# Seven products in place of eight for two token blocks of a second expert mixture

## The chip, the cores and the metric

One core of one Trainium2 chip runs the whole kernel in one launch. The metric is the device time in microseconds of a run; the kernel before has a median of 664.22 us over three runs (663.23 to 666.79).

## The reference

Three stages follow one another, in fp32. An attention with two kinds of masks (half of the heads local, half strided) gives 1152 tokens of 512 values. Then come two feed-forward mixtures:

```
h = np.maximum(x @ w_in, 0.0);  x = h * h @ w_out          # 512 -> 2048 -> 512, w_in and w_out given as float64
p = domain_probs / (domain_probs.sum(-1, keepdims=True) + 1e-09)
for e in range(4):                                        # 512 -> 1024 -> 512 for each expert
    h = np.maximum(x @ w1[e], 0.0)
    out += p[:, e:e + 1] * (h @ w2[e])
```

The second mixture runs all four experts on all tokens, so it is four dense feed-forward layers. Its first products, `x @ w1[e]`, are what the change works on.

## The kernel before

**Tiling.** The 1152 tokens are three blocks of `TB` = 384. Features are taken 128 at a time ("feature tile"); the 512 model values are `KD` = 4 contraction tiles of 128. A weight "unit" holds two feature tiles: for `w1` 512 x 256 values, for `w2` 256 x 512. An expert has four units of each.

**Precision.** Every operand is kept as a high and a low half (`fp32r` tiles of shape [128, 2, ...]); each product is three matmuls, high x high, high x low and low x high (`mm3`, lines 587 to 590). ScalarE makes the high half with a copy, VectorE the low half as value minus high half. For weights this is `hi` (L565) and `lo` (L569, on POOL for the first mixture and on VectorE for the second), for hidden tiles `hi` (L638) and `lo` (L641), which both read the accumulator tile of the first product and apply the ReLU.

**Order of the second mixture.** `steps` (line 258) lists expert, block and feature tile, with blocks in the order 2, 1, 0. One step is a first product, 4 contraction tiles x 3 matmuls of 384 columns into a tile `bh` of a ring of two (lines 606 to 618), then high and low half of the hidden tile. Two steps later (`LAG` = 2) comes its second product: for each of three groups of 128 tokens, three matmuls of 512 columns into accumulators `by`/`ba` that run over all eight feature tiles (lines 694 to 714, L710 to L712). Then VectorE adds the accumulator, times the expert's probability, into `acc` (`gather`, L723 and L725), and after the last expert the rows are stored. `RUN` = 2: two first products, then two second products, in turn.

```
steps += [(2, e, b, i) for e in range(E) for b in (2, 1, 0) for i in range(n2)]
r = (n - moe1) % RUN
return due(n - r) + 10 * r
```

**The end of the first mixture.** Its phases are `(block, half of the features)`; the last two are block 1 and block 0, second half. Their result is the sum of the accumulator and a `spill` tile of the first half (`both`, L679, written in place), and then `x` gets a high half (L684) and a low half (L687).

**What sets the order.** The class `Plan` takes every piece of work as a task with an engine, an estimated duration (`mm_r`, `act`, `dve`, `pool`, `dma`, lines 231 to 250), a rank, the tasks it comes after and the buffers that it takes from or gives back to rings. `run` (line 70) simulates the engines: whenever one is idle it starts the ready task of lowest rank whose buffers are free. The instructions are emitted in that order, each engine works its own list in that order, and the real waits are semaphores. All loads are issued from SP's queue. The weight ring `w` has 10 tiles and 3 more (`W_LATE`) when attention's memory is given up in `open_late` (line 504); the ring `raw` for loaded weights has 3.

Of the kernel before, what the change touches and what calls it, by code (L numbers as in the profile page):

```python
# [7 lines left out]
F32 = mybir.dt.float32  # L8
# [4 lines left out]
ALU = mybir.AluOpType  # L13
# [26 lines left out]
class Plan:  # L40
# [6 lines left out]

    SAME, CROSS, DMA = 100, 200, 2200
# [5 lines left out]
    def __init__(self):  # L54
        self.tasks, self.rings = [], {}
        self.filler = None

# [3 lines left out]
    def add(self, engines, emit, after=(), rank=0, take=(), free=(), adds=(), behind=None):  # L61
# [4 lines left out]
        t.number, t.begin, t.end, t.behind = len(self.tasks), None, None, behind  # L66
        self.tasks.append(t)
        return t

    def run(self):  # L70
# [21 lines left out]
        while done < len(self.tasks):  # L92
# [25 lines left out]
            for e in ready:  # L118
                while idle[e] and ready[e]:
                    held, got = [], None  # L120
                    while ready[e]:
                        item = heapq.heappop(ready[e])
                        t = item[2]
                        if t.begin is not None:
                            continue
                        if all(any(self.rings[r] for r in rings) for _, _, rings in t.take):
                            got = t
                            break
                        held.append(item)
# [27 lines left out]
def tile_attention_mlp_experts(ctx: ExitStack, tc: tile.TileContext, a, out):  # L157
# [7 lines left out]
    banks = ctx.enter_context(tc.tile_pool(name="banks", bufs=1, space=PSUM))  # L165
    attn = ExitStack()
# [3 lines left out]
    def f32(x):  # L170
        return x.bitcast(F32)

# [23 lines left out]
    RUN = 2  # L196
# [7 lines left out]
    W_EARLY, W_LATE = 10, 3  # L204
# [7 lines left out]
    spill = many(main, "y", NB - 1, [P, KD, TB])  # L212
    plan.ring("w", many(main, "w", W_EARLY, [P, 2, 4 * CH], F32R))
    plan.ring("raw", many(main, "raw", NRAW, [P, 4 * CH], U32))
    plan.ring("mid", many(main, "mid", NMID, [P, 2 * CH]))
    plan.ring("val", many(main, "val", NMID, [P, 2 * CH]))
    plan.ring("hid", many(main, "h", NHID, [P, 2, TB], F32R))
    plan.ring("r", many(main, "r", 2, [P, TB]))
# [20 lines left out]

    def act(n):  # L240
        return n + 40
# [16 lines left out]
    steps += [(2, e, b, i) for e in range(E) for b in (2, 1, 0) for i in range(n2)]  # L258
    n_steps = len(steps)
# [5 lines left out]
    grouped = moe1 + RUN  # L265

    def turn(n):

        r = (n - moe1) % RUN
        return due(n - r) + 10 * r  # L270

    def in_unit(st, e, i):
        return ("wi" if st == 1 else "w1", e, i * P // CH)

    def out_unit(st, e, i):
        return ("wo" if st == 1 else "w2", e, i * P // CH)
# [227 lines left out]
    def open_late(e):  # L504
# [3 lines left out]
        for s in range(W_LATE):  # L508
            late["w", s] = lp.tile([P, 2, 4 * CH], F32R, name=f"wl{s}")

    t_late = plan.add({"none": 1}, open_late, after=attention_done, rank=0, adds=[("w", [("w", s) for s in range(W_LATE)])])


    first, last_use = {}, {}
    for n, (st, e, b, i) in enumerate(steps):
        for u, k in ((in_unit(st, e, i), n), (out_unit(st, e, i), n + LAG)):
            first.setdefault(u, k)
            last_use[u] = n
    w_env, w_ready = {}, {}

    def weights(u):
        env = w_env[u]
        w = env["w"]
        return late[w] if isinstance(w, tuple) else w

    chain = {"dma": None, "w": None}
    for u in sorted(first, key=lambda x: first[x]):
# [3 lines left out]
        rank = due(first[u]) - (CONV0 if first[u] <= LAG else CONV)  # L531
        for j in range(2):
# [39 lines left out]
            if first[u] > LAG or wide_:  # L572
                chain["dma"] = t
# [6 lines left out]
            t = plan.add({"act": act(n)}, hi, after=[t, chain["w"]], rank=rank + 2000, take=[(w_env[u], "w", ["w"])] if j == 0 else [])  # L580
            chain["w"] = t
            lo_engines = {"pool": pool(n)} if wide_ else {"dve": dve(n)}
            t = plan.add(lo_engines, lo, after=[t], rank=rank + R_LO, free=[(env, "val") if wide_ else (env, "raw")])
# [7 lines left out]

    spare = plan.rings["bank_y"].pop()
    phase_of = {p: k for k, p in enumerate(phases)}
    whole = {b: phase_of[b, 1] == phase_of[b, 0] + 1 for b in range(NB)}
    x2_ready = {}
    spilled = {}
    y_env = {}
    use = {}
    previous = previous_y = None
    for n in range(n_steps + LAG):  # L600
        if n < n_steps:
            st, e_, b, i = steps[n]
            env = use[n] = {}
            u = in_unit(st, e_, i)
            order = (2, 3, 0, 1)
            for pos, kk in enumerate(order):
                def product(e, env=env, u=u, b=b, i=i, kk=kk, pos=pos):
                    w = weights(u).rearrange("p s (k f) -> p s k f", k=KD)
# [3 lines left out]
                if st == 1:  # L612
                    x_in = x_ready[b, (0, 1) if kk < 2 else (2, 3)]
                else:
                    x_in = [x2_ready[b, kk]]
                freed = [(w_env[u], "w")] if pos == 3 and last_use[u] == n else []
                previous = plan.add({"pe": 3 * mm_r(TB)}, product, after=[previous if pos else None, *x_in, *w_ready[u]], rank=due(n) + pos * PE_SLICE if n < grouped else turn(n) + pos, behind=previous if n >= grouped else None, take=[(env, "H", ["bank_h"])] if pos == 0 else [], free=freed, adds=[("bank_y", [spare])] if n == 0 and pos == 0 else ())
            t = previous
            rank = due(n) - URGENT
            if st == 1:  # L620
                def relu(e, env=env):
                    nc.scalar.activation(out=env["r"], in_=env["H"][:, :TB], func=AF.Relu, scale=1.0 / WSCALE)  # L622

                def square(e, env=env):
                    h = env["H"][:, :TB]
                    nc.vector.scalar_tensor_tensor(out=h, in0=h, scalar=0.0, in1=env["r"], op0=ALU.max, op1=ALU.mult)  # L626

                def hi(e, env=env):
                    nc.scalar.activation(out=env["hid"][:, 0], in_=env["H"][:, :TB], func=AF.Copy)  # L629

                def lo(e, env=env):
                    nc.vector.tensor_tensor(out=env["hid"][:, 1], in0=env["H"][:, :TB], in1=f32(env["hid"][:, 0]), op=ALU.subtract)  # L632

                t = plan.add({"act": act(TB)}, relu, after=[t], rank=rank, take=[(env, "r", ["r"])])
                t = plan.add({"dve": dve(TB)}, square, after=[t], rank=rank, free=[(env, "r")])
            else:
                def hi(e, env=env):
                    nc.scalar.activation(out=env["hid"][:, 0], in_=env["H"][:, :TB], func=AF.Relu)  # L638

                def lo(e, env=env):  # L640
                    nc.vector.scalar_tensor_tensor(out=env["hid"][:, 1], in0=env["H"][:, :TB], scalar=0.0, in1=f32(env["hid"][:, 0]), op0=ALU.max, op1=ALU.subtract)  # L641

# [5 lines left out]
        st, e_, b, i = steps[n]  # L648
        env = use[n]
        u = out_unit(st, e_, i)  # L650
        rank = due(n + LAG) + R_OUT
        freed_w = [(w_env[u], "w")] if last_use[u] == n else []
        if st == 1:
            hh = i // half
            start = i == (0 if whole[b] else hh * half)
            stop = i == n1 - 1 or (not whole[b] and i == half - 1)
            for d in range(KD):
                if start:
                    y_env[d] = {}

                def product(e, env=env, u=u, i=i, d=d, y=y_env[d], start=start, stop=stop):
                    w = weights(u).rearrange("p s (k f) -> p s k f", k=2)
                    cs = slice(d * P, (d + 1) * P)
                    mm3(y["y"][:, :TB], w[:, 0, i % 2, cs], w[:, 1, i % 2, cs], env["hid"][:, 0], env["hid"][:, 1], start, stop)

                freed = [(env, "hid"), *freed_w] if d == KD - 1 else []
                t = previous_y = plan.add({"pe": 3 * mm_r(TB)}, product, after=[env["ready"], previous_y, *w_ready[u]], rank=rank + d * PE_SLICE, take=[(y_env[d], "y", ["bank_y"])] if start else [], free=freed)
                if not stop:
                    continue
                y = y_env[d]  # L670
                if hh == 0:
                    def keep(e, b=b, d=d, y=y):
                        nc.scalar.activation(out=spill[b][:, d], in_=y["y"][:, :TB], func=AF.Copy)

                    spilled[b, d] = plan.add({"act": act(TB)}, keep, after=[t], rank=rank, free=[(y, "y")])
                    continue
                if not whole[b]:
                    def both(e, b=b, d=d, y=y):
                        nc.vector.tensor_tensor(out=y["y"][:, :TB], in0=y["y"][:, :TB], in1=spill[b][:, d], op=ALU.add)  # L679

                    t = plan.add({"dve": dve(TB)}, both, after=[t, spilled[b, d]], rank=rank)

                def hi(e, b=b, d=d, y=y):
                    nc.scalar.activation(out=xt[b][:, 0, d], in_=y["y"][:, :TB], func=AF.Copy, scale=1.0 / WSCALE**2)  # L684

# [139 lines left out]
```

## Time and profile before

| | |
|---|---|
| median of three runs | 664.22 us (663.23 to 666.79) |
| the profiled execution | 663.53 us |
| its span, first to last instruction | 661.8 us |
| TensorE busy | 648.0 us, 98% of the span, 3964 matmuls |
| VectorE, ScalarE, POOL busy | 278.7, 201.1, 57.7 us |
| granted TensorE clock, mean | 0.997 |
| moved over HBM | 42.13 MB read, 2.36 MB written |

How to read it: "busy" is the union of an engine's instructions in time. Matmuls overlap in the records (one of 384 columns has a duration of about 0.33 us and the next starts 0.17 us later), so the spacing of starts, not the duration, is what a matmul costs in a full stream. PEld is TensorE's loading of the stationary operand, which goes on beside it. A number behind an arrow names what ended an engine's idle time. Granted clock 1.00 is 2.4 GHz, the upper of TensorE's two levels; the lower is 1.2 GHz.

### The profile page before, as it was taken

How to read it: one execution, taken by the hardware profiler on the slowest of the kernel's cores; microseconds unless marked ns; L12 is line 12 of the kernel's file. 1: busy time of each engine (PE TensorE's matmuls, PEld its weight loads, DVE VectorE, ACT ScalarE, POOL GpSimd, SP SyncE). 2: the span in 40 equal slices, each digit the busy share in tenths (PEclk: the TensorE clock that was granted, in tenths of full speed). 3: DMA queues.
4: the chain of work that ended last, by engine and by line, in shares of the span. 5: the costliest groups of instructions: out<-in, count | busy, mean ns of one | idle time of the engine just before them, and what ended most of it. 6: DMA issues, size and time to landing. Idle time of an engine off the chain costs nothing.

```text
span 661.8 us, 9714 instructions
## 1 busy us (share of the span) xinstructions
PE 648.0 (98%) x3964; PEld 596.6 (90%) x3964; DVE 278.7 (42%) x506; ACT 201.1 (30%) x457; POOL 57.7 (9%) x55
## 2 busy tenths in 40 slices
PE   7898999999999999999999999999999999999998
PEld 4777889999999999999999999999999999999997
DVE  4898898775433464421344221343221232112122
ACT  2856676554322343211132111132111121111110
POOL 2445434330000000000000000000000000000000
PEclk9998999999999999999999999999999999999999
DMA  8975434334200122200132100033200000001011
GB/s 277 261 217 191 153 98 158 129 96 100 77 0 1 28 85 80 64 1 0 32 97 80 49 1 0 26 94 89 49 0 1 18 31 1 1 0 49 1 48 49
DMA packets 24636, 45.12 MB, mean 68 GB/s; under 512 B 4176, under 2 KB 9744, under 8 KB 24592
## 3 DMA queue, kind: packets, MB, share of 16 engines
q1 hardware_dynamic: 24592, 44.50, 22.1%
q8 instruction: 31, 0.51, 0.3%
q14 instruction: 13, 0.11, 0.1%
HBM read 42.13 MB, written 2.36 MB: 67 GB/s over the span
## 4 chain that ended last, share of the span: by engine, by line
PE 90%; DVE 4%; DMA 2%; ACT 1%; issue 1%; SPq 1%; POOL 0%; DVEq 0%; ACTq 0%; POOLq 0%
PE bh L588 15%; PE bh L589 15%; PE bh L590 15%; PE by L711 10%; PE by L712 10%; PE by L710 10%; PE by L588 5%; PE by L590 5%; PE by L589 5%; DVE val L550 1%; DMA pe<-in_pe_dram 1%; DMA q<-in_ql_dram 1%; DMA v<-in_vs_dram 1%; DVE val L554 1%; DVE val L559 1%
## 5 line engine op out<-in xcount | busy, mean ns | idle before, releaser
L641 DVE SCALAR_TENSOR_TENSOR h<-bh,h 128x384 fp32r<-128x384 f32 x96 | 53.5, 557 | 254.6 <-ACT h L638 254.5
L588 PE MATMUL bh<-x,w 128*128 128x384 f32 x432 | 146.7, 340 | 1.1 <-DVE h L632 1.1
L589 PE MATMUL bh<-x,w 128*128 128x384 f32 x432 | 145.1, 336 | 0.6 <-DVE x L486 0.6
L590 PE MATMUL bh<-x,w 128*128 128x384 f32 x432 | 145.2, 336 | 0.0
L638 ACT ACTIVATE h<-bh 128x384 fp32r<-128x384 f32 x96 | 47.1, 491 | 301.3 <-PE bh L590 300.7
L712 PE MATMUL by<-w,h 128*128 128x512 f32 (+1 forms) x242 | 93.2, 385 | 0.0
L711 PE MATMUL by<-w,h 128*128 128x512 f32 (+1 forms) x242 | 93.1, 385 | 0.0
L710 PE MATMUL by<-w,h 128*128 128x512 f32 (+1 forms) x242 | 92.4, 382 | 0.0
L588 PEld LDWEIGHTS bh<-x,w 128*128 128x128 f32 x432 | 81.5, 189 | 3.5 <-DVE h L632 1.7
L589 PEld LDWEIGHTS bh<-x,w 128*128 128x128 f32 x432 | 81.5, 189 | 2.1 <-DVE x L486 0.8
L590 PEld LDWEIGHTS bh<-x,w 128*128 128x128 f32 x432 | 81.3, 188 | 0.0
L588 PE MATMUL by<-h,w 128*128 128x384 f32 x168 | 57.5, 342 | 0.3 <-ACT h L629 0.3
L589 PE MATMUL by<-h,w 128*128 128x384 f32 x168 | 56.5, 336 | 0.6 <-DVE h L632 0.6
L590 PE MATMUL by<-h,w 128*128 128x384 f32 x168 | 56.5, 337 | 0.0
L712 PEld LDWEIGHTS by<-w,h 128*128 128x128 f32 x242 | 45.4, 188 | 8.9
L711 PEld LDWEIGHTS by<-w,h 128*128 128x128 f32 x242 | 45.4, 188 | 8.3
L710 PEld LDWEIGHTS by<-w,h 128*128 128x128 f32 x242 | 45.5, 188 | 8.1
L590 PE MATMUL bh<-x,wl 128*128 128x384 f32 x144 | 48.2, 335 | 0.0
L588 PE MATMUL bh<-x,wl 128*128 128x384 f32 x144 | 48.2, 335 | 0.0
L589 PE MATMUL bh<-x,wl 128*128 128x384 f32 x144 | 48.2, 335 | 0.0
L626 DVE SCALAR_TENSOR_TENSOR bh<-bh,r 128x384 f32<-128x384 f32 x48 | 27.0, 563 | 44.2 <-ACT r L622 44.1
L622 ACT ACTIVATE r<-bh 128x384 f32<-128x384 f32 x48 | 23.6, 491 | 63.7 <-PE bh L590 63.5
(103 smaller groups left out, 816.6 us busy)
## 6 DMA issues: line engine op xcount, KB each, us to landing
raw<-in_w_dram SPq DMA_DIRECT2D x64, 256.0 KB, 2.7
raw<-in_wi_dram SPq DMA_DIRECT2D x16, 512.0 KB, 3.7
raw<-in_wo_dram SPq DMA_DIRECT2D x16, 512.0 KB, 3.6
out_dram<-acc SPq DMA_DIRECT2D x8, 256.0 KB, 2.0
v<-in_vs_dram SPq DMA_DIRECT2D x6, 256.0 KB, 4.2
v<-in_vl_dram SPq DMA_DIRECT2D x8, 192.0 KB, 4.1
k<-in_kl_dram SPq DMA_DIRECT2D x8, 160.0 KB, 4.1
q<-in_ql_dram SPq DMA_DIRECT2D x8, 128.0 KB, 4.1
```

What stands on the lines that cost most here:

```text
L550: nc.vector.tensor_scalar(out=env["val"].bitcast(U32), in0=env["mid"].bitcast(U32), scalar1=3, scalar2=0x7FFFFFF8, op0=ALU.logical_shift_l ...
L554: nc.vector.scalar_tensor_tensor(out=v, in0=env["mid"].bitcast(U32), scalar=0x80000000, in1=v, op0=ALU.bitwise_and, op1=ALU.bitwise_or)
L588: nc.tensor.matmul(dst, lhsT=wh, rhs=xh, start=start, stop=False)
L589: nc.tensor.matmul(dst, lhsT=wh, rhs=xl, start=False, stop=False)
L590: nc.tensor.matmul(dst, lhsT=wl, rhs=xh, start=False, stop=stop)
L622: nc.scalar.activation(out=env["r"], in_=env["H"][:, :TB], func=AF.Relu, scale=1.0 / WSCALE)
L626: nc.vector.scalar_tensor_tensor(out=h, in0=h, scalar=0.0, in1=env["r"], op0=ALU.max, op1=ALU.mult)
L638: nc.scalar.activation(out=env["hid"][:, 0], in_=env["H"][:, :TB], func=AF.Relu)
L641: nc.vector.scalar_tensor_tensor(out=env["hid"][:, 1], in0=env["H"][:, :TB], scalar=0.0, in1=f32(env["hid"][:, 0]), op0=ALU.max, op1=ALU.s ...
L710: nc.tensor.matmul(o, lhsT=h[:, 0, ts], rhs=w[:, 0], start=start, stop=False)
L711: nc.tensor.matmul(o, lhsT=h[:, 0, ts], rhs=w[:, 1], start=False, stop=False)
L712: nc.tensor.matmul(o, lhsT=h[:, 1, ts], rhs=w[:, 0], start=False, stop=stop)
```

## The change

Blocks 1 and 0 are taken together. With the unit's weights as a 2 x 2 matrix A (rows: its two feature tiles; columns: two halves of the 512 contraction values) and the two blocks of x as B (rows: the halves; columns: blocks 1 and 0), the four hidden tiles are the 2 x 2 product of A and B. They are made of seven products instead of eight, by Winograd's form of Strassen's scheme: the left sums S1 to S4 are sums of A's parts, the right sums T1 to T4 of B's, and seven additions combine the products. Block 2 stays as it was, by itself. An expert is now a single part (block 2) and a two-block part, single first for experts 0 to 2, two-block first for expert 3. Both kinds go in groups of four feature tiles: the first products of four, then the second products of four, with no lag. Left sums are made per unit: the unit is loaded a second time, POOL makes the four sums, ScalarE and VectorE their halves, into one of two buffers. Right sums are made once, after the first mixture; `acc` holds them meanwhile, and block 0's contraction half B12 no longer needs halves of its own. The weight ring stays at 10 tiles. Tasks marked `quiet` (weight conversions, left sums, gathers) are not started on an engine while a group's products hold that engine "tense". The plan's estimate of a matmul grows by 10 ns (`mm_s`).

```diff
+                        if not (t.quiet and e in self.tense) and all(any(self.rings[r] for r in rings) for _, _, rings in t.take):
...
+                    self.tense |= set(got.tenses)
+                    self.tense -= set(got.relaxes)
...
-    RUN = 2
+    GROUP = 4
-    W_EARLY, W_LATE = 10, 3
+    NW = 10
+    NS = 2
+    NTMP = 3
+    S_LEAD = 16000
...
-    steps += [(2, e, b, i) for e in range(E) for b in (2, 1, 0) for i in range(n2)]
+    pair = (1, 0)
+    alone = 2
+    IN, IN7, OUT = 3 * KD * mm_s(TB), 42 * mm_s(TB), 9 * mm_s(DM)
+    for e_, two in [(e, two) for e in range(E) for two in ((False, True) if e < E - 1 else (True, False))]:
+        for g in range(n2 // 2 if two else n2 // GROUP):
+            t_in = now
+            t_out = now = now + (IN7 if two else GROUP * IN)
+            now += GROUP * OUT
...
+            t = plan.add({"dve": dve(TB)}, diff, after=[*x2_wide.values(), t_late, *t_sums], rank=rank)
+            t = plan.add({"act": act(TB)}, hi, after=[t, previous], rank=rank)
+            t_ready[n].append(plan.add({"dve": dve(TB)}, lo, after=[t], rank=rank))
...
+        def s1(e, env=env, part=part):
+            nc.gpsimd.tensor_tensor(out=got(env["sf"])[:, 0], in0=part(env, 1, 0), in1=part(env, 1, 1), op=ALU.add)
...
+        t = t_load = plan.add({"dma": dma(P * 4 * CH * 4)}, load, after=[t_load], rank=rank - FETCH, take=[(env, "raw", ["raw"]), (env, "S", ["sums"])])
+        for k, emit in enumerate((s1, s2, s3, s4)):
+            t = plan.add({"pool": pool(hk * P)}, emit, after=[t], rank=rank, take=[(env, "sf", ["parts"])] if k == 0 else [], free=[(env, "raw")] if k == 3 else [], quiet=True)
...
+                t = seven("P1", A11, B11, tenses=("act",))
+                p1 = on_act(lambda e, c=c: nc.scalar.activation(out=got(c["c11"]), in_=c["P1"][:, :TB], func=AF.Copy), [t], take=taken("c11", "tmp"), free=[(c, "P1")])
+                t = seven("P6", S2, T2, tenses=("dve", "pool"))
+                u2 = on_dve(add("c12", "P6", "c11"), [t, p1], take=taken("c12", "tmp"), free=[(c, "P6")])
+                t = seven("P2", A12, B21)
+                c11 = on_dve(add("c11", "P2", "c11"), [t, u2], free=[(c, "P2")])
+                t = seven("P7", S3, T3)
+                u3 = on_dve(add("c21", "P7", "c12"), [t, u2], take=taken("c21", "tmp"), free=[(c, "P7")], relaxes=("pool",))
+                t = seven("P5", S1, T1)
+                p5 = on_act(lambda e, c=c: nc.scalar.activation(out=got(c["c22"]), in_=c["P5"][:, :TB], func=AF.Copy), [t], take=taken("c22", "tmp"), free=[(c, "P5")])
+                u4 = on_dve(add2("c12", "c12", "c22"), [u3, p5])
+                c22 = on_dve(add2("c22", "c22", "c21"), [u4], relaxes=("dve",))
+                t = seven("P4", A22, T4, free=[(w_env[u], "w")] if last_part[u] == (e_, two) else [])
+                c21 = on_dve(add("c21", "P4", "c21"), [t, c22], free=[(c, "P4")])
+                t = seven("P3", S4, B22, free=[(s_env[un], "S")])
+                c12 = on_dve(add("c12", "P3", "c12"), [t, u4], free=[(c, "P3")])
+                for key, t, b, r in (("c11", c11, 1, 0), ("c22", c22, 0, 1), ("c21", c21, 1, 1), ("c12", c12, 0, 0)):
...
+                    t = on_act(hi, [t], take=[(env, "hid", ["hid"])], relaxes=("act",) if key == "c22" else ())
+                    env["ready"] = on_dve(lo, [t, u3], free=[(c, key)])
```

`seven` emits the six matmuls of one product (two contraction tiles x `mm3`) into a tile of the ring `bank_h`, which still has two; `add` is an addition of a product in that tile and an SBUF tile, `add2` of two SBUF tiles; `c11` to `c22` are SBUF tiles of 128 x 384. The high and low half of a hidden tile of blocks 1 and 0 now read such an SBUF tile. The second products of a group's four tiles follow in the order c11, c22, c21, c12.

## Rows read from the trace of the kernel before

**Rows 1.** Page, part 1: busy us (share of the span) x instructions.

```profile
PE 648.0 (98%) x3964; PEld 596.6 (90%) x3964; DVE 278.7 (42%) x506; ACT 201.1 (30%) x457; POOL 57.7 (9%) x55
```

**Rows 2.** Page, part 4: the chain that ended last, by engine.

```profile
PE 90%; DVE 4%; DMA 2%; ACT 1%; issue 1%; SPq 1%; POOL 0%; DVEq 0%; ACTq 0%; POOLq 0%
```

**Rows 3.** Stretches: PE, PEld, DVE, ACT, POOL busy (instructions), clock, DMA share, GB/s.

```profile
150.00:200.00 50.00, 50.00 (x290) 50.00 (x290) 21.89 (x38) 18.30 (x38) 0.75 (x1) 1.00 0.21 58
...
239.00:272.00 33.00, 33.00 (x187) 32.26 (x185) 18.05 (x32) 13.99 (x28) 0.00 (x0) 1.00 0.32 100
272.00:305.00 33.00, 33.00 (x168) 30.07 (x168) 6.57 (x11) 3.94 (x8) 0.00 (x0) 1.00 0.04 11
338.00:371.00 33.00, 33.00 (x168) 30.07 (x168) 13.63 (x22) 9.87 (x19) 0.00 (x0) 1.00 0.33 101
```

**Rows 4.** Page, part 5: first products, one of three lines; busy, mean ns, idle before.

```profile
L588 PE MATMUL bh<-x,w 128*128 128x384 f32 x432 | 146.7, 340 | 1.1 <-DVE h L632 1.1
...
L588 PE MATMUL bh<-x,wl 128*128 128x384 f32 x144 | 48.2, 335 | 0.0
```

**Rows 5.** Timeline, PE: start us, duration us; starts of runs.

```profile
254.71 0.33 PE L588 MATMUL bh<-x,w 128*128 128x384 f32 x1
...
261.99 0.33 PE L588 MATMUL bh<-x,w 128*128 128x384 f32 x1
...
400.61 0.39 PE L710 MATMUL by<-wl,h 128*128 128x512 f32 x1
...
404.73 0.33 PE L588 MATMUL bh<-x,w 128*128 128x384 f32 x1
...
408.92 0.39 PE L710 MATMUL by<-w,h 128*128 128x512 f32 x1
```

**Rows 6.** Timeline: from a tile's last matmul to its halves; a release of PE.

```profile
82.55 0.55 DVE L632 TENSOR_TENSOR h<-bh,h 128x384 fp32r<-128x384 f32 x1
...
83.15 0.44 PE L588 MATMUL bh<-x,w 128*128 128x384 f32 x1 [0.90 <-DVE h L632]
...
408.75 0.33 PE L590 MATMUL bh<-x,w 128*128 128x384 f32 x1
...
409.12 0.49 ACT L638 ACTIVATE h<-bh 128x384 fp32r<-128x384 f32 x1 [1.59 <-PE bh L590]
...
409.64 0.56 DVE L641 SCALAR_TENSOR_TENSOR h<-bh,h 128x384 fp32r<-128x384 f32 x1 [1.52 <-ACT h L638]
```

**Rows 7.** Groups by line and form: count, busy us, mean ns, idle before.

```profile
L569 DVE TENSOR_TENSOR w<-raw,w 128x512 fp32r<-128x512 f32 x50 | 35.0, 703 | 16.5 <-ACT w L565 16.5
L569 POOL TENSOR_TENSOR w<-val,w 128x512 fp32r<-128x512 f32 x26 | 34.7, 1340 | 46.5 <-ACT w L565 43.8 <-PE by L589 2.7
...
L565 ACT ACTIVATE w<-raw 128x512 fp32r<-128x512 f32 x50 | 30.9, 626 | 16.5 <-PE bh L589 10.8 <-PE by L712 5.7
...
L679 DVE TENSOR_TENSOR by<-by,y 128x384 f32<-128x384 f32 x8 | 4.5, 562 | 1.8 <-PE by L590 1.8
...
L473 POOL TENSOR_TENSOR p<-p,st 128x192 f32<-128x192 f32 x2 | 1.0, 512 | 4.5 <-ACT pt L453 2.5 <-DVE st L472 2.0
```

**Rows 8.** Two lines of VectorE: count, duration ns min/median/max, first and last start.

```profile
L559 DVE SCALAR_TENSOR_TENSOR val<-raw,val x32: 641/692/1665, 16.6 to 148.0; 128x512 uint32<-128x512 uint32 x32
...
L626 DVE SCALAR_TENSOR_TENSOR bh<-bh,r x48: 550/566/567, 37.7 to 252.9; 128x384 f32<-128x384 f32 x48
```

**Rows 9.** Timeline, POOL and VectorE at the same time.

```profile
106.94 1.66 POOL L569 TENSOR_TENSOR wl<-val,wl 128x512 fp32r<-128x512 f32 x1 [1.43 <-ACT wl L565]
107.36 0.56 DVE L626 SCALAR_TENSOR_TENSOR bh<-bh,r 128x384 f32<-128x384 f32 x1
107.83 1.32 DVE L559 SCALAR_TENSOR_TENSOR val<-raw,val 128x512 uint32<-128x512 uint32 x1
```

**Rows 10.** Page, part 6: a load of 512 KB, median us from issue to landing.

```profile
raw<-in_wi_dram SPq DMA_DIRECT2D x16, 512.0 KB, 3.7
```

**Rows 11.** Timeline, the last instruction on VectorE.

```profile
658.49 0.48 DVE L725 SCALAR_TENSOR_TENSOR acc<-by,pe,acc 128x256 f32<-128x256 f32 x1 [0.23 <-PE by L712]
```

More of the change, by code (lines that the diff above doesn't have):

```diff
@@ L56, in __init__, with add @@
         self.filler = None
+        self.tense = set()
     def ring(self, name, tiles):
         self.rings[name] = list(tiles)
-    def add(self, engines, emit, after=(), rank=0, take=(), free=(), adds=(), behind=None):
+    def add(self, engines, emit, after=(), rank=0, take=(), free=(), adds=(), behind=None, quiet=False, tenses=(), relaxes=()):
         t = Plan.Task()
@@ L507, in open_late @@
         late["acc"] = lp.tile([P, NT // P, DM], F32, name="acc")
[L508 to L516, printed above, removed]
+        for k in range(3):
+            late["T", k] = lp.tile([P, 2, KD // 2, TB], F32R, name=f"t{k}")
+        late["parts", 0] = lp.tile([P, 4, 2, P], F32, name="sf")
+        late["tmp", 0] = lp.tile([P, TB], F32, name="c0")
+    t_late = plan.add({"none": 1}, open_late, after=attention_done, rank=0)
+    first, last_use, when = {}, {}, {}
+    for n, (_, _, b, i) in enumerate(steps):
+        for u, k in ((("wi", 0, i // 2), n), (("wo", 0, i // 2), n + LAG)):
             first.setdefault(u, k)
+            when.setdefault(u, due(k))
             last_use[u] = n
+    when.update({u: t for u, t in need.items() if u[0] != "s1"})
     w_env, w_ready = {}, {}
     def weights(u):
-        env = w_env[u]
-        w = env["w"]
-        return late[w] if isinstance(w, tuple) else w
+        return w_env[u]["w"]
     chain = {"dma": None, "w": None}
-    for u in sorted(first, key=lambda x: first[x]):
+    for u in sorted(when, key=lambda x: when[x]):
         kind, e_, c = u
@@ L530, in tile_attention_mlp_experts @@
         wide_ = kind in ("wi", "wo")
-        rank = due(first[u]) - (CONV0 if first[u] <= LAG else CONV)
+        soon = wide_ and first[u] <= LAG
+        rank = when[u] - (CONV0 if soon else CONV)
         for j in range(2):
@@ L616, in tile_attention_mlp_experts @@
                 freed = [(w_env[u], "w")] if pos == 3 and last_use[u] == n else []
-                previous = plan.add({"pe": 3 * mm_r(TB)}, product, after=[previous if pos else None, *x_in, *w_ready[u]], rank=due(n) + pos * PE_SLICE if n < grouped else turn(n) + pos, behind=previous if n >= grouped else None, take=[(env, "H", ["bank_h"])] if pos == 0 else [], free=freed, adds=[("bank_y", [spare])] if n == 0 and pos == 0 else ())
+                previous = plan.add({"pe": 3 * mm_r(TB)}, product, after=[previous if pos else None, *x_ready[b, (0, 1) if kk < 2 else (2, 3)], *w_ready[u]], rank=due(n) + pos * PE_SLICE, take=[(env, "H", ["bank_h"])] if pos == 0 else [], free=freed, adds=[("bank_y", [spare])] if n == 0 and pos == 0 else ())
@@ L618, in tile_attention_mlp_experts @@
             t = previous
             rank = due(n) - URGENT
[L620 to L641, printed above, removed]
@@ L643, in tile_attention_mlp_experts @@
+            t = plan.add({"act": act(TB)}, relu, after=[t], rank=rank, take=[(env, "r", ["r"])])
+            t = plan.add({"dve": dve(TB)}, square, after=[t], rank=rank, free=[(env, "r")])
             t = plan.add({"act": act(TB)}, hi, after=[t], rank=rank, take=[(env, "hid", ["hid"])])
@@ new lines, in open_last @@
+    def open_last(e):
+        early.close()
+        rp = ctx.enter_context(tc.tile_pool(name="last", bufs=1, side="right"))
+        for k in range(NS):
+            late["sums", k] = rp.tile([P, 2, 4, hk, P], F32R, name=f"s{k}")
+        for k in range(NTMP):
+            late["tmp", k + 1] = rp.tile([P, TB], F32, name=f"c{k + 1}")
+    t_last = plan.add({"none": 1}, open_last, after=[*t_sums, *(t for u in w_ready if u[0] in ("wi", "wo") for t in w_ready[u])], rank=0, adds=[("sums", [("sums", k) for k in range(NS)]), ("parts", [("parts", 0)]), ("tmp", [("tmp", k) for k in range(NTMP + 1)])])
@@ new lines, in tile_attention_mlp_experts, with on_pe, gather_store, gather @@
+    nt = TB // P
+    last_pe = None
+    def on_pe(cost, emit, rank, after, **more):
+        nonlocal last_pe
+        last_pe = plan.add({"pe": cost}, emit, rank=rank, after=[last_pe, *after], behind=last_pe, **more)
+        return last_pe
+    def gather_store(b, t_, e_, y, cs, t, rank):
+        g = b * nt + t_
+        def gather(e):
+            o, acc, pcol = y["y"][:, : cs.stop - cs.start], late["acc"][:, g, cs], pe[:, g, e_ : e_ + 1]
+            if e_ == 0:
+                nc.vector.tensor_scalar(out=acc, in0=o, scalar1=pcol, scalar2=None, op0=ALU.mult)
+            else:
+                nc.vector.scalar_tensor_tensor(out=acc, in0=o, scalar=pcol, in1=acc, op0=ALU.mult, op1=ALU.add)
+        def store(e):
+            nc.sync.dma_start(out=out[g * P : (g + 1) * P, cs], in_=late["acc"][:, g, cs])
+        t = plan.add({"dve": dve(cs.stop - cs.start)}, gather, after=[t, t_pe, *t_sums, *(x for n in t_ready for x in t_ready[n])], rank=rank - URGENT, free=[(y, "y")], quiet=True)
+        if e_ == E - 1:
+            plan.add({"dma": dma(P * (cs.stop - cs.start) * 4)}, store, after=[t], rank=rank)
@@ new lines, in second_product, with product @@
+    def second_product(env, u, r, y, t_, cs, start, stop):
+        def product(e):
+            w = w_out(u)[:, :, r, cs]
+            ts = slice(t_ * P, (t_ + 1) * P)
+            h, o = env["hid"], y["y"][:, : w.shape[-1]]
+            nc.tensor.matmul(o, lhsT=h[:, 0, ts], rhs=w[:, 0], start=start, stop=False)
+            nc.tensor.matmul(o, lhsT=h[:, 0, ts], rhs=w[:, 1], start=False, stop=False)
+            nc.tensor.matmul(o, lhsT=h[:, 1, ts], rhs=w[:, 0], start=False, stop=stop)
+        return product
```

311 lines of the change are left out of this document (210 added, 101 removed).

## The prediction

> **What bounds the kernel now.** I read the page's busy times first: TensorE is busy 98% of the span, every other engine 42% or less [rows 1]. The chain that ended last then says the same by another road: 90% of it is PE [rows 2]. Third, the busy times in stretches of 33 us: in the second mixture PE is busy 33.00 of 33.00 us and issues 168 matmuls in each, whether VectorE works 6.57 or 13.63 us beside it, and the granted clock is 1.00, the upper of its two levels, 2.4 GHz [rows 3]. The stretch from 150 to 200 us, in the first mixture, is as full [rows 3]. So there nothing is waited for; the time is a count of matmuls times their spacing, and other engines matter only when they make PE wait.
>
> The spacing comes from starts in the timeline [rows 5]. In the first mixture 42 matmuls of 384 columns lie between 254.71 and 261.99: 0.1733 us each. In the second, 18 matmuls of 512 columns take 400.61 to 404.73, 0.2289 each, and 24 of 384 take 404.73 to 408.92, 4.19 us, which is 24 x 0.1733 + 0.03. I read the 0.03 as the price of changing from one kind to the other.
>
> **What is removed.** First products are 576 per source line over both mixtures [rows 4], three lines, 12 per feature tile and token block. For two blocks and one unit (two feature tiles) that is 48 matmuls; the scheme needs 7 products x 2 contraction tiles x 3 = 42. Sixteen units (4 experts x 4) save 96 matmuls: 96 x 0.1733 = 16.6 us. Runs of one kind number 48 before and 24 after (16 two-block groups, 8 single groups), 24 x 0.03 = 0.7 us more. Second products keep their number. All of it is on the path, because PE has no idle time there: **17.3 us**. A two-block group is then 42 x 0.1733 + 0.03 + 36 x 0.2289 = 15.55 us, against 2 x 8.31 = 16.62 before.
>
> **What is added beside PE.** Per group VectorE does seven combining operations of 0.56 (priced by the addition L679 [rows 7]) and the four low halves at 0.56 as before: 11 x 0.56 = 6.2 us; the low halves of the left sums, 2 x 0.70 = 1.4; and up to two units of weights, 4 x 0.70 = 2.8 [rows 7]. That is 10.4 of 15.55 us. ScalarE: two copies and four high halves of 0.49 [rows 6], 2 + 4 operations of 0.63 [rows 7], 6.7 us. POOL has no row for a 256-column sum; 192 columns took 0.51 and 512 took 1.34 [rows 7], so I take 0.7 (ends 0.51 and 1.34), 2.8 us a group. None of these is on the path as long as each result is there in time, which is the real question.
>
> **The two banks of the seven products.** One product is 6 x 0.1733 = 1.04 us, and the product after the next needs its bank. From the rows [rows 6]: the last matmul of a tile starts at 408.75, so the next run starts at 408.92; ScalarE starts at 409.12, 0.20 later, takes 0.49, VectorE follows 0.03 later; a VectorE end at 83.10 lets PE start at 83.15, 0.05 later. So a bank is emptied 0.20 + 0.56 + 0.05 = 0.81 us after its product by VectorE, 0.74 by ScalarE: 0.23 and 0.30 us to spare. Five products per group (all but the first two) reuse a bank. I take no stall. Ends: 0, and all five late by 0.2, 16 us in all; no gain can lie here, since PE can't go faster than its spacing. What keeps VectorE free for it is the new rule of the plan that holds conversions, left sums and gathers back while the chain runs.
>
> **The hidden tiles.** Count from the end of the fourth product (P7). P5 ends at 1.04, its copy at 1.73; the two SBUF additions run to 2.32 and 2.88; the second tile's high half ends at 3.40; the additions for P4 and P3 go first and end at 4.00; its low half ends at 4.56. P3 ends at 3.12 and nine second products on the first tile (2.06) hide the rest to 5.18: 0.6 us to spare. The third and fourth tiles (5.12, 5.68) have over 2 us. Cost nothing.
>
> **Left sums and their transfers.** Each is another 512 KB from SP; such a load lands in 3.7 us [rows 10]. It waits for one of two sum buffers, freed when P3 ends, so it lands at 3.12 + 3.7 = 6.8 on the same count, POOL ends at 9.6, VectorE a little later, and the sums are needed only after one whole further group. Behind the waiting load on SP stand weight loads, and behind those the conversions; for experts 0 to 2 the two-block part uses units that the single part already brought, so nobody waits. The weight ring falls from 13 tiles to 10: eight are held by an expert, and each group frees two 15.55 us before two more are wanted. Cost nothing; if that cover is gone, a late unit costs at most its load and conversions, about 2.7 + 1.4 us once.
>
> **The turn between the mixtures.** The right sums are 8 differences and 8 low halves on VectorE, 16 x 0.56 = 9.0 us, and 8 copies on ScalarE; block 0 saves two of each half. They are needed only after the first single part (two groups, 33 us), in which VectorE had 6.57 us of work and 18.05 in the stretch before [rows 3]. But they crowd: about 15 us of work falls in the first 16. There a tile's bank must be free within a product of 12 x 0.1733 = 2.08 us, and emptying takes 0.20 + 0.49 + 0.03 + 0.56 + 0.05 = 1.33, 0.75 to spare; a low half behind three sums is 1.7 late, about 1 us of stall. **I take 1 us**, ends 0 and 3. The first 250 us keep their work, and the tail from the last matmul over gather and store [rows 11] keeps its form.
>
> **Sum.** The profiled execution took 663.53 us (span 661.8, 1.7 around it), 0.7 under the median of 664.22. 663.53 - 17.3 + 1.0 = **647.2 us**.
>
> **A row that speaks against it.** POOL's sums meet VectorE. At 106.94 a POOL operation started and ran 1.66 us, to 108.60; a VectorE operation with two inputs in SBUF that started at 107.83 took 1.32 us and ended 0.55 after POOL did, while one with a PSUM input, at 107.36, took its usual 0.56 [rows 9]. Over the run the first kind reaches from 641 to 1665 ns, the second only from 550 to 567 [rows 8]. The Trainium skill, "SBUF — State Buffer", section "Who interferes with whom", states this as a rule: a VectorE instruction with two SBUF inputs and a GpSimd instruction that reads SBUF exclude each other, and whichever comes second waits for the whole of the first. By that rule the trace agrees. By the placement worked out above (POOL from 6.8 to 9.6) the two don't meet in the chain and the sum stays 647.2; where they meet, it is the second rival.
>
> **Rivals.**
> First, **crowding**: the turn, or weight units that come late with ten tiles, cost 3 to 9 us instead of 1. For it: the plan reckons VectorE's operations shorter than they are (470 against 557 ns for 384 columns), so a crowded stretch runs behind its plan. Against it: VectorE has 40% of the time free. 650 to 656 us, chance 0.12.
> Second, **the shared access decides**, on the other side: the sums run late (the raw ring has three tiles for all loads) and POOL works from the end of the third addition on, under the two SBUF additions and the low halves, which now read SBUF alone. Three operations stand before the second hidden tile; each waiting 0.7 us gives 2.1, less the 0.6 to spare: PE waits 1.5 us per group, 16 x 1.5 = 24, and the time is 671. It decides once a group waits over 16.3 / 16 = 1.0 us. Against it: the plan holds POOL back up to that addition, and the buffers allow the sums earlier. Chance 0.07.
> Third, **the banks**: the 0.23 us isn't there, five products each late by 0.2, 16 us lost, 663, about no change. For it: no stretch of the kernel before empties a bank in every microsecond; the nearest does it every 2.08. Against it: the rows above. Chance 0.06.
>
> **How the numbers follow.** The forecast has 0.75 with a range of its own of 645 to 650 (no stall at all, or 3 us at the turn). The 8-in-10 range reaches over the first rival, 645 to 656, which leaves out the second and third. A measurement here tells about 0.5%, 3.3 us. Faster: 0.75 + 0.12 = 0.87; same 0.06, the third rival; slower 0.07, the second.
>
> **What would show it.** Right: 3868 matmuls instead of 3964; PE busy without idle time through the two-block parts, groups of 15.5 us apart; combining operations of 0.56 us starting 0.20 after their product; no PE wait on them. Wrong: PE waits on an addition (banks), on a low half in the second products (shared access, with VectorE operations of over 1 us beside POOL), or on weights and sums at a part's start; a lower granted clock; a 384-column spacing other than 0.173.

## The result, and the profile after

The changed kernel takes 647.27 us (median of four runs, 646.02 to 650.45) against 663.73 for the kernel before (four runs beside it): 0.975 of the time, 95% interval 0.9704 to 0.9796. The forecast was 647.2 us.

The page of the profiled execution (647.54 us, span 645.8), parts 1 and 4, answers to [rows 1, 2]:

```profile
PE 631.5 (98%) x3868; PEld 580.2 (90%) x3868; DVE 360.8 (56%) x664; ACT 235.6 (36%) x527; POOL 105.9 (16%) x119
...
PE 88%; DVE 5%; ACT 2%; DMA 2%; issue 1%; POOL 1%; SPq 1%; DVEq 0%; ACTq 0%; POOLq 0%
```

TensorE has 3868 matmuls, 96 fewer, and is as full as before. VectorE works 82 us more, ScalarE 35 and POOL 48, and the chain is still PE. The stretches (columns as in [rows 3]) show the same in the second mixture:

```profile
272.00:305.00 33.00, 33.00 (x168) 29.95 (x167) 18.20 (x32) 9.76 (x19) 5.76 (x8) 1.00 0.19 52
...
536.00:569.00 33.00, 33.00 (x168) 30.11 (x167) 24.28 (x42) 11.65 (x23) 10.37 (x12) 1.00 0.17 56
```

VectorE is busy 18.20 us of 33 where it was 6.57, in the fullest stretch 24.28, and TensorE has no idle time in either. The list of waits has no wait of PE at all between 268 and 645 us.

Where the time went is read from starts of runs of matmuls in the timeline (as [rows 5]):

```profile
268.95 0.39 PE L834 MATMUL by<-w,h 128*128 128x512 f32 x1
...
277.16 0.33 PE L617 MATMUL bh<-x,w 128*128 128x384 f32 x1
...
285.50 0.39 PE L834 MATMUL by<-w,h 128*128 128x512 f32 x1
...
293.70 0.33 PE L617 MATMUL bh<-x,w 128*128 128x384 f32 x1
...
301.07 0.39 PE L834 MATMUL by<-w,h 128*128 128x512 f32 x1
...
309.27 0.33 PE L617 MATMUL bh<-x,w 128*128 128x384 f32 x1
...
642.20 0.28 PE L836 MATMUL by<-w,h 128*128 128x256 f32 x1
```

Line 834 is a second product of 512 columns, line 617 a first product of 384. A single group takes 268.95 to 285.50, 16.55 us; a two-block group 293.70 to 309.27, 15.57; the same four tiles took 16.62 before. So 16 x 1.05 + 8 x 0.07 = 17.4 us should be gone. As a whole: at the first run of 512 columns, both kernels have done the first mixture and four tiles of the second. From there to the start of the last matmul it is 268.95 to 642.20 = **373.25 us** after, and 390.47 before, by the two rows that follow. The second mixture is 17.22 us shorter. This length repeats to 0.01 us between profiled executions of one kernel, while what lies ahead of it differs (268.95 us in this execution, 269.73 in the next), so the experiments are read by it too.

The kernel before, the same two places of the timeline:

```profile
267.70 0.39 PE L710 MATMUL by<-w,h 128*128 128x512 f32 x1
...
658.17 0.28 PE L712 MATMUL by<-w,h 128*128 128x256 f32 x1
```

But that first run starts 1.25 us later than before, so the profiled executions differ by 16.0 and not by 17.2. The loss lies in the first mixture. From the first ScalarE operation after 105 us that opens a hidden tile there (106.76 before, 106.45 after) to that run it is 160.94 us before and 162.50 after, 1.56 more. One idle time of PE, before 145.48 (waits in brackets), makes 0.61 of it; the rest has no idle time in the records, and the stretches show where it begins. After:

```profile
106.45 0.49 ACT L650 ACTIVATE r<-bh 128x384 f32<-128x384 f32 x1 [1.33 <-PE bh L619]
...
110.00:120.00 10.00, 10.00 (x60) 10.00 (x59) 2.73 (x5) 3.02 (x6) 0.00 (x0) 1.00 0.12 48
120.00:130.00 10.00, 10.00 (x59) 10.00 (x58) 3.20 (x6) 3.65 (x8) 2.21 (x2) 1.00 0.00 0
...
140.00:150.00 10.00, 9.39 (x53) 8.86 (x53) 9.14 (x15) 5.14 (x11) 3.09 (x3) 1.00 0.35 108
...
145.48 0.44 PE L617 MATMUL bh<-x,w 128*128 128x384 f32 x1 [0.61 <-DVE h L660]
```

Before, the same places:

```profile
106.76 0.47 ACT L622 ACTIVATE r<-bh 128x384 f32<-128x384 f32 x1
...
110.00:120.00 10.00, 10.00 (x59) 10.00 (x58) 7.95 (x13) 5.01 (x10) 3.76 (x3) 1.00 0.45 159
120.00:130.00 10.00, 10.00 (x60) 10.00 (x59) 7.79 (x14) 5.81 (x11) 3.84 (x3) 1.00 0.39 114
...
140.00:150.00 10.00, 10.00 (x59) 10.00 (x58) 7.17 (x13) 5.65 (x12) 3.14 (x3) 1.00 0.23 56
```

From 110 to 130 us VectorE now does 2.73 and 3.20 us of work per 10 where it did 7.95 and 7.79, and no load runs at 120 to 130; from 140 on it is busy 9.14 of 10 and a low half comes late for PE. Something holds the first mixture's weight conversions back.

A two-block group's chain on VectorE and ScalarE, beside a few rows of PE, from the timeline of the same execution (872: addition of a product; 893: copy; 875: SBUF additions; 907: low halves):

```profile
296.08 0.56 DVE L872 TENSOR_TENSOR c<-bh,c 128x384 f32<-128x384 f32 x1 [1.42 <-PE bh L619]
...
296.33 0.33 PE L617 MATMUL bh<-x,w 128*128 128x384 f32 x1
...
296.85 0.34 PE L617 MATMUL bh<-t,s 128*128 128x384 f32 x1
...
297.05 0.56 DVE L872 TENSOR_TENSOR c<-bh,c 128x384 f32<-128x384 f32 x1 [0.42 <-PE bh L619]
...
297.89 0.34 PE L617 MATMUL bh<-t,s 128*128 128x384 f32 x1
...
298.10 0.56 DVE L872 TENSOR_TENSOR c<-bh,c 128x384 f32<-128x384 f32 x1 [0.49 <-PE bh L619]
...
299.14 0.49 ACT L893 ACTIVATE c<-bh 128x384 f32<-128x384 f32 x1 [0.92 <-PE bh L619]
...
299.67 1.15 DVE L875 TENSOR_TENSOR c<-c,c 128x384 f32<-128x384 f32 x2 [0.55 <-ACT c L893]
...
300.93 1.02 DVE L872 TENSOR_TENSOR c<-bh,c 128x384 f32<-128x384 f32 x2
...
301.87 0.55 DVE L907 SCALAR_TENSOR_TENSOR h<-c,h 128x384 fp32r<-128x384 f32 x1
...
303.15 0.39 PE L834 MATMUL by<-w,h 128*128 128x512 f32 x1
...
303.38 0.19 PEld L836 LDWEIGHTS by<-w,h 128*128 128x128 f32 x1
...
306.92 0.74 POOL L779 TENSOR_TENSOR sf<-raw 128x256 f32<-128x256 f32 x1 [18.48 <-issue]
```

The first three additions come about one microsecond apart, each waiting for PE and not PE for it; the last two follow the SBUF additions without a wait. P7 runs from 296.85 to 297.89. The second tile's low half ends at 302.42, and the second products on it start nine matmuls after 301.07, at 303.15: 0.73 us to spare where 0.6 was reckoned. In fact there is more, since the first two of each three matmuls read the high half alone: the low half is first read by the third's weight load, at 303.38, 0.96 us later. POOL starts at 306.92, long after the chain.

### The profile page after: what moved, and what is told of

It is laid out like the page before. It is cut to its first block, busy times and chain, and to the rows that moved or that the text cites. A ratio compares the mean times of both kernels' runs of the same rounds, so it can differ in the third digit from the quotient of the medians.

```text
span 645.8 us, 9891 instructions
## 1 busy us (share of the span) xinstructions
PE 631.5 (98%) x3868; PEld 580.2 (90%) x3868; DVE 360.8 (56%) x664; ACT 235.6 (36%) x527; POOL 105.9 (16%) x119
## 4 chain that ended last, share of the span: by engine, by line
PE 88%; DVE 5%; ACT 2%; DMA 2%; issue 1%; POOL 1%; SPq 1%; DVEq 0%; ACTq 0%; POOLq 0%
PE bh L617 14%; PE bh L618 14%; PE bh L619 14%; PE by L835 8%; PE by L836 8%; PE by L834 8%; PE by L617 5%; PE by L619 4%; PE by L618 4%; PE ba L836 2%; PE ba L835 2%; PE ba L834 2%; DVE val L580 1%; DVE val L589 1%; DVE val L584 1%
## 5 line engine op out<-in xcount | busy, mean ns | idle before, releaser
L617 PE MATMUL bh<-x,w 128*128 128x384 f32 x416 | 141.8, 341 | 1.7 <-DVE h L660 1.7
L619 PE MATMUL bh<-x,w 128*128 128x384 f32 x416 | 139.8, 336 | 0.0
L618 PE MATMUL bh<-x,w 128*128 128x384 f32 x416 | 139.7, 336 | 0.0
L872 DVE TENSOR_TENSOR c<-bh,c 128x384 f32<-128x384 f32 x80 | 43.1, 556 | 85.9 <-ACT c L885 58.4
L836 PE MATMUL by<-w,h 128*128 128x512 f32 (+1 forms) x232 | 89.0, 384 | 0.0
L835 PE MATMUL by<-w,h 128*128 128x512 f32 (+1 forms) x232 | 89.0, 384 | 0.0
L834 PE MATMUL by<-w,h 128*128 128x512 f32 (+1 forms) x232 | 88.5, 382 | 0.0
L617 PEld LDWEIGHTS bh<-x,w 128*128 128x128 f32 x416 | 78.5, 189 | 4.7 <-DVE h L660 3.2
L618 PEld LDWEIGHTS bh<-x,w 128*128 128x128 f32 x416 | 78.5, 189 | 1.0
L619 PEld LDWEIGHTS bh<-x,w 128*128 128x128 f32 x416 | 78.4, 188 | 0.0
L779 POOL TENSOR_TENSOR sf<-raw 128x256 f32<-128x256 f32 x16 | 12.1, 755 | 347.1 <-DMA raw<-in_w_dram 283.8
L617 PE MATMUL by<-h,w 128*128 128x384 f32 x192 | 65.5, 341 | 0.3 <-ACT h L657 0.3
L618 PE MATMUL by<-h,w 128*128 128x384 f32 x192 | 64.5, 336 | 0.6 <-DVE h L660 0.6
L619 PE MATMUL by<-h,w 128*128 128x384 f32 x192 | 64.6, 336 | 0.0
L599 POOL TENSOR_TENSOR w<-val,w 128x512 fp32r<-128x512 f32 x32 | 43.3, 1361 | 76.4 <-ACT w L595 73.9
L929 DVE SCALAR_TENSOR_TENSOR h<-bh,h 128x384 fp32r<-128x384 f32 x32 | 17.8, 557 | 64.0 <-ACT h L926 64.0
L904 ACT ACTIVATE h<-c 128x384 fp32r<-128x384 f32 x64 | 31.8, 518 | 54.6 <-DVE c L872 34.5
L599 DVE TENSOR_TENSOR w<-raw,w 128x512 fp32r<-128x512 f32 x64 | 43.1, 696 | 9.3 <-ACT w L595 9.3
```

What stands on the lines that cost most here:

```text
L599: eng[e].tensor_tensor(out=w[:, 1, cs], in0=value(), in1=f32(w[:, 0, cs]), op=ALU.subtract)
L617: nc.tensor.matmul(dst, lhsT=wh, rhs=xh, start=start, stop=False)
L618: nc.tensor.matmul(dst, lhsT=wh, rhs=xl, start=False, stop=False)
L619: nc.tensor.matmul(dst, lhsT=wl, rhs=xh, start=False, stop=stop)
L779: nc.gpsimd.tensor_tensor(out=got(env["sf"])[:, 0], in0=part(env, 1, 0), in1=part(env, 1, 1), op=ALU.add)
L834: nc.tensor.matmul(o, lhsT=h[:, 0, ts], rhs=w[:, 0], start=start, stop=False)
```

## The experiments

Ten runs. Lengths of the second mixture are taken as above. The changed kernel itself ran again beside the next three: 

> The changed kernel again, beside the three runs that follow. Theory: 647.3 us. In its profile the stretch from 110 to 165 us should again lose about 1.5 us of TensorE time against the kernel before, and the second mixture again have no idle TensorE.

 Measured: 648.31 us, ratio 0.9748 (0.9723 to 0.9773), second mixture 373.24 us, PE busy 9.39 of 10 at 140 to 150 us again. Both readings above repeat.

**Undo the seven products alone.** All blocks in groups of four with eight products; the parts' loop runs over blocks, the sums go:

```diff
-    for e_, two in [(e, two) for e in range(E) for two in ((False, True) if e < E - 1 else (True, False))]:
+    for e_, blk in [(e, b) for e in range(E) for b in (2, 1, 0)]:
```

> Groups of four kept, ten weight tiles kept, but all three blocks by eight products (no sums, no combining additions). Theory (the gain is 96 matmuls of 0.1733 us): 16.6 us come back, 647.3 + 16.6 = 663.9 us. Rival (the gain is the new order in groups of four): under 655 us.

Measured: 663.61 us, ratio 0.9993 (0.9974 to 1.0013), so the whole gain is gone. Its profile:

```profile
273.80 0.39 PE L830 MATMUL by<-w,h 128*128 128x512 f32 x1
...
662.78 0.28 PE L832 MATMUL by<-w,h 128*128 128x256 f32 x1
```

That is 388.98 us. The seven products give 388.98 - 373.25 = 15.7 us of the 17.2, and the groups of four 390.47 - 388.98 = 1.5. In the total these 1.5 us are offset by the first mixture, which loses time here as well, with PE idle for 0.6 us before 150.34, though this run has no sums and no combining additions.

**The ring of ten, put into the kernel before.**

```diff
-    W_EARLY, W_LATE = 10, 3
+    W_EARLY, W_LATE = 10, 0
```

> The kernel before with ten weight tiles instead of thirteen, nothing else. Theory (the ten tiles hold back the first mixture's conversions, which then crowd at 130 to 150 us): 1.2 to 1.6 us slower than the kernel before, lost between 110 and 165 us. Rival (the loss there comes from something else in the change): within 0.5 us of the kernel before.

Measured: 665.63 us (12 runs), ratio 1.0023 (1.0004 to 1.0041). The loss is measured free of what lies ahead by the ScalarE operation that opens each hidden tile of the first mixture: from the first one after 105 us to the last there are 36 in the kernels compared here. In the kernel before they span 145.60 us, here 147.02, in the changed kernel 147.16. The second mixture keeps 390.46. The first of the 36, a thin stretch as in the changed kernel, and the first run of 512 columns:

```profile
107.48 0.49 ACT L622 ACTIVATE r<-bh 128x384 f32<-128x384 f32 x1 [1.31 <-PE bh L590]
...
110.00:120.00 10.00, 10.00 (x60) 10.00 (x59) 2.25 (x4) 2.53 (x5) 0.00 (x0) 1.00 0.20 54
...
269.84 0.39 PE L710 MATMUL by<-w,h 128*128 128x512 f32 x1
```

From the first to the last of these it is 162.36 us, 1.42 more than the 160.94 of the kernel before. So the ten tiles cost 1.4 us in the first mixture and nothing in the second, with no sums in the kernel at all.

**Give the tiles back where they are missed.** The memory that the right sums and `acc` take after the first mixture holds three more weight tiles until then, for the first mixture alone:

```diff
+        wp = lent.enter_context(tc.tile_pool(name="lent", bufs=1))
+        for k in range(NLENT):
+            late["wl", k] = wp.tile([P, 2, 4 * CH], F32R, name=f"wl{k}")
+    def open_late2(e):
+        lent.close()
         lp = ctx.enter_context(tc.tile_pool(name="late", bufs=1))
...
-            t = plan.add({"act": act(n)}, hi, after=[t, chain["w"]], rank=rank + 2000, take=[(w_env[u], "w", ["w"])] if j == 0 else [], quiet=not wide_)
+            t = plan.add({"act": act(n)}, hi, after=[t, chain["w"]], rank=rank + 2000, take=[(w_env[u], "w", ["wl", "w"] if wide_ else ["w"])] if j == 0 else [], quiet=not wide_)
```

(The second expert's loads also wait for the loads of the first two units of left sums, since the ring `raw` would otherwise fill with them.)

> The changed kernel, with three more weight tiles lent to the first mixture in the memory that the sums and the accumulators take afterwards. Theory: the 1.5 us between 110 and 165 us come back, 645.8 us, and the second mixture keeps its length. Rival: 647.3 us, because the loss has another cause.

Measured: 646.88 us, ratio 0.9736 (0.971 to 0.9763); the 36 tiles take 145.95 us and the second mixture 373.25. The first of the 36, the stretches, and the first run of 512 columns:

```profile
107.84 0.47 ACT L662 ACTIVATE r<-bh 128x384 f32<-128x384 f32 x1
...
110.00:120.00 10.00, 10.00 (x59) 10.00 (x59) 7.66 (x13) 5.31 (x10) 3.91 (x3) 1.00 0.43 125
...
140.00:150.00 10.00, 10.00 (x59) 10.00 (x59) 7.63 (x13) 4.58 (x10) 2.60 (x2) 1.00 0.21 69
...
268.78 0.39 PE L849 MATMUL by<-w,h 128*128 128x512 f32 x1
```

VectorE is back at its even load and PE has no idle time. The last of the 36 tiles moves by some tenths by itself; from the first tile to the run of 512 columns it is 160.94 us, as in the kernel before, so all of the 1.56 us is back. Beside the changed kernel's 648.31 us on the same chip the total is lower too, but the two intervals overlap: the gain is shown by this stretch rather than by the totals. Five lent tiles: 

> Five tiles lent to the first mixture instead of three. Theory (three already leave no idle TensorE from 110 to 170 us): no further gain, 646.9 us within 1, the second mixture 373.2 us. Rival (weights still come late somewhere): 1 us or more faster.

 Measured: 647.18 us, ratio 0.975 (0.9724 to 0.9776), 36 tiles in 145.58 us, second mixture 373.35. From the first tile (108.13) to the run of 512 columns (269.06) it is 160.93 us: nothing more, as expected.

**Double the additions that free a bank.**

```diff
+                def twice(key, bank, other, c=c):
+                    def emit(e):
+                        nc.vector.tensor_tensor(out=late["twice"], in0=c[bank][:, :TB], in1=got(c[other]), op=ALU.add)
+                        nc.vector.tensor_tensor(out=got(c[key]), in0=c[bank][:, :TB], in1=got(c[other]), op=ALU.add)
...
-                u2 = on_dve(add("c12", "P6", "c11"), [t, p1], take=taken("c12", "tmp"), free=[(c, "P6")])
+                u2 = on_dve(twice("c12", "P6", "c11"), [t, p1], take=taken("c12", "tmp"), free=[(c, "P6")])
```

The additions for P2 and P7 are changed in the same way.

> The three additions that free a bank which the same group needs again (after P6, P2 and P7) are done twice, 0.56 us more each. Theory (0.23 us to spare per bank): TensorE waits 0.33, 0.08 and 0.25 us per group, and up to 0.1 for each restart, 16 x 0.66 to 0.95 = 10.6 to 15 us, 658 to 662 us. Rival (banks have more room than reckoned): under 650 us.

Measured: 660.26 us, ratio 0.9937 (0.9916 to 0.9958). Timeline, PE and its weight loads: the group's start, the second half of P2, the start of P7 with its wait, and the next group's start:

```profile
294.35 0.33 PE L617 MATMUL bh<-x,w 128*128 128x384 f32 x1
...
296.98 0.33 PE L617 MATMUL bh<-x,w 128*128 128x384 f32 x1
...
297.80 0.19 PEld L617 LDWEIGHTS bh<-t,s 128*128 128x128 f32 x1 [0.46 <-DVE c L878]
297.80 0.45 PE L617 MATMUL bh<-t,s 128*128 128x384 f32 x1
...
310.64 0.33 PE L617 MATMUL bh<-x,w 128*128 128x384 f32 x1
```

P7 starts 0.82 us after P2's second half instead of 0.52 (296.33 to 296.85 in the changed kernel), on the addition that frees its bank. The group takes 294.35 to 310.64, 16.29 us, 0.72 more; the second mixture 385.36, 12.1 more. The bank has the room that was reckoned and no more: 0.56 us more on it is paid for.

**POOL under the chain.** The first form only changed the plan's order: the next unit's sums come after the third addition (`s_first["s1", e_, g + 1].after.append(u3)`). 

> POOL's four sums for the next unit are made to wait for the third addition of the group before, so that they run under the SBUF additions and the low halves (12 of 16 groups). Shared access decides: VectorE operations with two SBUF inputs take over 1 us there, the second hidden tile is 1.5 us late, 12 x 1.5 = 18 us, 665 us. Theory that the slack covers it: such operations are seen, but TensorE doesn't wait, 647 to 649 us.

 Measured: 649.29 us, ratio 0.9769 (0.973 to 0.9808), second mixture 373.54. The 0.3 us more lie in one group, in which the first addition begins 0.4 us late, at 584.06, and P7 waits for its bank; why is open. On the shared access it told nothing, because POOL's real waits are on data alone, and its sums still ran after the chain. So the order was bound by data:

```diff
+            if u in s_after:
+                nc.gpsimd.tensor_tensor(out=got(env["sf"])[:, 0, 0], in0=got(s_after[u]["c21"])[:, :P], in1=got(s_after[u]["c21"])[:, :P], op=ALU.add)
```

> As the run with POOL's sums under the additions, but bound by data this time: before the four sums of the next unit POOL first reads the result of the third addition (one small operation of 128 columns more), in 12 of 16 groups. Shared access decides: the sums then run from about 0.9 to 4.5 us after the fourth product, the SBUF additions and the second tile's low half each wait for one of them, the second hidden tile comes 0.8 to 1.5 us late, 12 x 0.8 to 1.5 = 10 to 18 us more, second mixture 383 to 391 us instead of 373.2. Slack covers it: VectorE operations of over 0.6 us are seen there, but the second mixture stays at 373 to 374 us.

Measured: 649.0 us, ratio 0.978 (0.9746 to 0.9814), second mixture 269.60 to 643.43 = 373.83. Its timeline (878: the two SBUF additions, 875: additions of a product, 913: low half):

```profile
315.02 0.58 POOL L780 TENSOR_TENSOR sf<-c 128x128 f32<-128x128 f32 x1 [11.46 <-DVE c L875]
...
315.68 0.74 POOL L781 TENSOR_TENSOR sf<-raw 128x256 f32<-128x256 f32 x1
...
315.96 1.89 DVE L878 TENSOR_TENSOR c<-c,c 128x384 f32<-128x384 f32 x2 [0.61 <-ACT c L899]
...
316.51 0.94 POOL L784 TENSOR_TENSOR sf<-sf,raw 128x256 f32<-128x256 f32 x1
...
317.40 1.06 POOL L787 TENSOR_TENSOR sf<-raw 128x256 f32<-128x256 f32 x1
...
317.99 1.02 DVE L875 TENSOR_TENSOR c<-bh,c 128x384 f32<-128x384 f32 x2
...
318.42 0.73 POOL L790 TENSOR_TENSOR sf<-raw,sf 128x256 f32<-128x256 f32 x1
...
318.93 0.65 DVE L913 SCALAR_TENSOR_TENSOR h<-c,h 128x384 fp32r<-128x384 f32 x1
...
319.36 0.39 PE L837 MATMUL by<-w,h 128*128 128x512 f32 x1
...
319.63 0.19 PEld L839 LDWEIGHTS by<-w,h 128*128 128x128 f32 x1
```

Now they meet. The two SBUF additions take 1.89 us instead of 1.15 and the low half 0.65 instead of 0.55, POOL's second and third sums 0.94 and 1.06 instead of 0.74, the additions with a PSUM input their usual time. The second tile's low half ends at 319.58. Its second products start at 319.36, and the weight load that first reads the low half could start 0.23 later, at 319.59, as at 303.38 in the changed kernel. It starts at 319.63, 0.05 us after the low half's end, which is the release time of [rows 6]: PE's load does wait for the low half here, but by a few hundredths, and the group's 36 second products take 8.22 us (317.28 to 325.50) instead of 8.20. Over twelve groups that makes 0.3 of the 0.6 us; the rest lies in one group, in which the first addition begins late as in the run before. So the slack of 0.96 us covers the meeting almost exactly, and nothing of it is left.

**Without the plan's hold.** `t.quiet` is False for every task. 

> The plan no longer holds conversions, left sums and gathers back while a group's products run. Theory: an operation of 0.69 us ahead of an addition makes a bank up to 0.46 us late, some such hits per group, 2 to 8 us in all, 649 to 655 us. Rival (the plan's ranks suffice without the rule): 647 us.

 Measured: 648.67 us, ratio 0.9758 (0.972 to 0.9796), second mixture 373.24, that of the changed kernel. The expected loss didn't come. In 11 of the 16 groups a weight conversion does get into the chain, but only behind the two SBUF additions (the first at 302.52, for 0.69 us), where the slack of the low half covers it, and never ahead of an addition that frees a bank the group needs again; so the ranks suffice. **Side work left out.** 

> Left sums are made for the first expert alone; the other three use two of them again. That leaves out 12 of 16 transfers of 512 KB, 48 POOL sums, 24 operations of ScalarE and 24 of VectorE. Theory (all of it is hidden): 647.3 us, within 1. Rival (side work slows TensorE's stream): 2 us faster or more.

 Measured: 648.77 us, ratio 0.9772 (0.9727 to 0.9816), second mixture 373.24. What twelve units cost in transfers, sums and halves is hidden to 0.01 us.

## Why the prediction was right

- **The bound.** Right: PE has no idle time in the second mixture with 82 us more on VectorE, and leaving side work out gains nothing there.
- **What is removed, 17.3 us.** Measured 17.22. The two parts were off by nearly as much each, in opposite ways, which is luck: the 96 matmuls gave 15.7 for 16.6, the groups of four 1.5 for 0.7. The change back to second products costs time as well, which the prediction had inside its 0.2289: 36 in a row took 8.20 us (285.50 to 293.70), where two runs of 18 took 2 x 4.12, so that 24 changes to and fro fewer gave 1.49 / 24 = 0.06 each. And the 42 matmuls of a two-block group took 7.37 us, not 7.31, while 48 in a single group took 8.34, as reckoned. The 0.06 is not at the run's start: in the group shown the first four products took 4.19 us (293.70 to 297.89), which is 24 x 0.1733 + 0.03, and the last three 3.18 (to 301.07), 1.06 each for 1.04. Why they are slower, without an idle time, stays open; 16 x 0.06 is about what the 96 matmuls gave less.
- **A two-block group, 15.55 us.** Measured 15.57, by the same two errors: 0.06 more in the first products, 0.04 less in the second.
- **Banks and hidden tiles, no stall.** Right, and the room was the reckoned one: additions doubled by 0.56 us cost 0.72 a group where 0.66 to 0.95 was expected.
- **Left sums.** They ran later than reckoned (POOL at 306.92, 9.0 us after P7's end and not 6.8), still clear of the chain. The reason given for VectorE being free, the plan's hold, was wrong: without it the length is the same.
- **The turn, 1 us.** Wrong: from the last hidden tile of the first mixture to the first run of 512 columns both kernels take 15.34 us, and behind that PE has no idle time, so nothing was lost there.
- **"The weight ring falls from 13 tiles to 10 ... Cost nothing."** Wrong by 1.4 to 1.6 us. The sentence looked at the second mixture alone, where it holds; the three tiles were missed in the first, whose second half of weights could no longer be converted ahead (the thin stretches at 110 to 130 us) and then came in a crowd. "The first 250 us keep their work" was true of the work and not of its times.

The last two errors cancel, 1 us taken and not paid, 1.5 paid and not taken; without that luck the forecast would have been 646.2 or 648.7, both within the range. Two medians of the changed kernel, 647.27 and 648.31, lie 1 us apart themselves, so agreement to a tenth is luck in any case. Of the rivals, crowding came in the first mixture and not at the turn, and at 1.5 us for 3 to 9; the banks and the shared access are real mechanisms, as two runs show, but the change as it is reaches neither. The shared access was priced too high: three operations at 0.7 us made 2.1, where the bound run lost 0.74 on the two additions and 0.10 on the low half, and the low half is wanted 0.23 later than reckoned.

## What to carry to other kernels

Where one engine has no idle time, a change is worth about the count of its instructions times their spacing (15.7 us here for a count of 16.6), and work put on the others is free until a buffer's return is late; so reckon each return against the time between two uses, and test the room by doubling the operation. When a buffer ring is cut, follow it through every stage that takes from it, not only through the stage that is changed. A plan's order is not a wait: an engine with nothing else in its queue starts as soon as its data are there.

## What the runs showed of the hardware

Where VectorE operations with two SBUF inputs met POOL in the bound run, they lost no more than what was left of POOL's operation, not the whole of it. The first addition began 0.28 us after a POOL operation of 0.74 and lost 0.32 us, with 0.46 of that operation left; the low half lost 0.10 with 0.22 left (318.93 against 318.42 + 0.73). The two additions, 0.88 and 0.98 us long, lost 0.74 us together. The delay goes both ways, POOL's next two operations took 0.94 and 1.06 us. The Trainium skill, "SBUF — State Buffer", section "Who interferes with whom", calls the lock on the shared ports exclusive, by which the second to start waits for the first. The run agrees in kind, with waits shorter than the rest of the first operation; what I had not expected is how little it comes to when both engines take turns.

In all twelve bound groups the weight load that first reads the low half starts 0.05 to 0.06 us after the low half's end (319.58 and 319.63 above). So an operand that is loaded as a weight is wanted with the load and not with its matmul, here 0.23 us earlier.
